# Attention by hash buckets with adapters: the last two pairs of heads interleaved by thirds of the queries, and a first pair prepared in another order

## The chip, the cores and the metric

The kernel runs on one core of a Trainium2 chip. The metric is the device time of one execution in microseconds (us). Eight runs of the kernel before are shown, and their median counts.

## What is computed

The first half is attention in which a query sees only the keys of its own hash bucket; the second half sends each row through two of eight small adapters and adds the result.

```python
q_bits = (np.einsum('bhsd,dk->bhsk', q, proj) > 0)       # 6 bits; the same for k
mask = q_bucket[:, :, :, None] == k_bucket[:, :, None, :]
scores = np.where(mask, scale * (q @ k.T), -1e9)
attn = softmax(scores); x = attn @ v                     # (4, 8, 768, 64) -> (3072, 512)
logits = x @ w_gate                                      # 8 experts, the best two, softmax over them
out = x + sum over the two experts e of w[e] * (x @ A[e]) @ B[e]     # rank 16
```

There are 4 batches of 8 heads, 768 positions and 64 features per head.

## The kernel before, in words

**Pairs and slots.** Two heads of a batch make a pair; there are 16 pairs (0 to 15), four to a batch. For each pair the scores are computed with the keys on the partitions, so that the exp of a score tile P is at once the stationary operand of the product with v. 2 heads x 6 key tiles x 768 queries are 9216 columns, cut into nine slots of 1024. `score` (L316) does one slot: three or four matmuls into a tile of the pool `ps_s` (two buffers of two PSUM banks), and one exp on ScalarE into `P_[p]`.

**The mask without a mask.** `aug` (L89, one of two buffers, alternating by pair) has 71 rows: 64 features, six signs of plus or minus one half, and one constant. Planes j = 0 to 3 are queries of head 0, keys of head 0, queries of head 1, keys of head 1. The score matmul over 71 rows falls far below zero wherever a bit differs; a small uniform term stands for rows that find no key (`uniform`, L354, with VectorE's add in `norm`, or for the last four pairs a matmul with the constant tile `eps`, L340).

**Preparing a pair.** `load_qk` and `load_v` queue loads on SyncE (SP). `trans` (L228) turns four blocks of 128x128 on TensorE into a PSUM bank and VectorE (or ScalarE) evicts them to `qkT`. `hash` (L252) makes the hash of all four planes in four column groups, VectorE takes the signs, and `sign_dma` (L163) moves them to rows 64 to 69 of `aug` by a transfer from SP's queue, one for each plane. `cast` (L272) fills rows 0 to 63 on GpSimd.

**Products.** `pvmm` (L334) multiplies P by v, six matmuls for each of six query tiles of a head, into a bank of `ps_v` (two banks); `norm` divides by the row sums and writes `x`, and GpSimd casts it to `xb`. `xturn` turns `xb` by a transfer, `xtrans` (L449) on TensorE with a copy on VectorE or ScalarE.

**Adapters.** `lgz` gives logits and the eight projections, `route_a` the maximum and the difference, `route_e` the exp of the router on ScalarE, `route_b` the weights and their product with the projections, `zmtrans` a transpose, `delta` the product with B, the sum with x and the store. `delta` ends either on VectorE or, with `by_pool`, on ScalarE (`tmp`) and GpSimd. A batch's six row tiles are done while the pairs of the next batch run; `moe_group` (L559) says which in which pair, `moe_slot` in which slot. For batch 2 they are (0, 1, 2) in pair 13 and (3, 4, 5) in pair 14.

**Order.** The whole order is written out by hand: the tile framework adds the waits between engines, but every engine runs its instructions as they are listed. `prologue` (L67) does head 0 and head 1 of pair 0, `first_pair` (L601) what lies beside its nine slots, `pair` (L630) what lies beside the slots of pairs 1 to 14, `last_pair` (L672) pair 15 and the tail. In pair 0, head 0's signs are written straight into `aug` by VectorE (`signs0`, L134), head 1's by `hash0` and two transfers. Pair 15's score columns are ordered so that two query tiles of both heads (a third of its queries) are complete after three slots; `third` (L389) does their product. The last third is done in two sixths after the last exp.

**Pools of one bank.** `ps_t` and `ps_m` have one bank each: an instruction that writes a new tile there waits until the last reader of the tile before is done.

Of the kernel before, what the change touches and what calls it, by code (L numbers as in the profile page):

```python
# [19 lines left out]
class Emitter:  # L20
# [46 lines left out]
    def prologue(self):  # L67
# [25 lines left out]
        self.qkT[0] = self.qktp.tile([P, 2 * S], F32, tag="qkT", name="qkT0")  # L93
        self.warm(19)
        self.turn0(0, self.ps_s, "s")
        self.half0(0, 0, nc.scalar.copy)
        self.half0(0, 1, nc.scalar.copy)
        self.signs0()
        self.turn0(1, self.ps_v, "v")
# [3 lines left out]
        self.half0(1, 0, nc.gpsimd.tensor_copy)  # L103
        self.half0(1, 1, nc.gpsimd.tensor_copy)
# [15 lines left out]
    def turn0(self, h, pool, tag):  # L120
        nc, P = self.nc, self.P
        for i in range(2):
            ps = pool.tile([P, 384], F32, tag=tag, name=f"trf{h}_{i}")
            for u in range(3):
                nc.tensor.transpose(out=ps[:, u * P:(u + 1) * P],  # L125
                                    in_=self.nat[0][:, i, h, u * P:(u + 1) * P], identity=self.ident)
            out = self.qkT[0][:, (2 * h + i) * 384:(2 * h + i + 1) * 384]
            if i:
# [5 lines left out]
    def signs0(self):  # L134
        nc, P = self.nc, self.P
        for i in range(2):
            hs = self.ps_s.tile([P, 2, 512], F32, tag="s", name=f"hsd{i}")
            for e in range(2):
                nc.tensor.matmul(out=hs[64:70, e, 0:384], lhsT=self.pst[64 * e:64 * e + 64, :],  # L139
                                 rhs=self.qkT[0][64 * e:64 * e + 64, i * 384:(i + 1) * 384],  # L140
                                 start=True, stop=True)
            nc.vector.tensor_scalar(out=self.aug[0][64:70, i, :].rearrange("p (e c) -> p e c", e=2),
                                    in0=hs[64:70, :, 0:384], scalar1=0.0, scalar2=0.5,
                                    op0=ALU.is_gt, op1=ALU.subtract)

    def hash0(self, h, engs):
        nc = self.nc
        hs = self.ps_t.tile([self.P, 384], F32, tag="t", name=f"hsf{h}")
        rows = slice(64 * h, 64 * h + 64)
        for i in (2 * h, 2 * h + 1):  # L150
            nc.tensor.matmul(out=hs[32 * i:32 * i + 32, :], lhsT=self.proj2,
                             rhs=self.qkT[0][:, i * 384:(i + 1) * 384], start=True, stop=True)
# [622 lines left out]
```

## Time and profile before

| | |
|---|---|
| median of 8 runs | 176.48 us (175.41 to 178.53) |
| profiled execution | 176.11 us, its span 174.3 us |
| granted TensorE clock | 0.988 |
| busy, TensorE and ScalarE | 161.9 and 150.8 us |
| busy, VectorE and GpSimd | 116.1 and 115.6 us |
| DMA | 28.51 MB, 164 GB/s on the mean |

A line of the page's groups has the source line, the engine, the operation, output and input with their shapes and the count, then the busy time, the mean of one in ns, and the idle time just before it with what ended it. A line of the timeline has start and duration in us, and merges equal instructions (x3) that follow each other; the idle time before the first stands in brackets. The span of 174.3 us ends with the landing of the last store.

### The profile page before, as it was taken

To read this page: it belongs to the slowest core of one execution; us is meant where nothing else is said; L and a number is where in the kernel's file an instruction comes from. 1 tells how busy PE (TensorE), PEld (TensorE's weight loads), DVE (VectorE), ACT (ScalarE), POOL (GpSimd) and SP (SyncE) were. 2 spreads that over 40 slices of the span, in tenths; PEclk is the share of its full clock that TensorE was granted. 3 is DMA by queue.
4 is the path that set the end of the run, shared out by engine and by line. 5 is a ranking of instruction groups with operands and counts; after the bars stand their busy time and mean duration, and the time that the engine had idled before them with its cause. 6 is when DMAs were issued, how large, how long until landed. Compare 5 with 4: busy or idle time off the path is not lost.

```text
span 174.3 us, 5249 instructions
## 1 busy us (share of the span) xinstructions
PE 161.9 (93%) x2100; PEld 112.1 (64%) x2105; DVE 116.1 (67%) x312; ACT 150.8 (87%) x176; POOL 115.6 (66%) x140
## 2 busy tenths in 40 slices
PE   7987999999999999999999999999999999998840
PEld 6454767675757676767667686767677676687610
DVE  3661747474746787878687786878785676647870
ACT  3666999999998899999997999999997988997760
POOL 8289969797897657575756677576766476630180
PEclk9999999999999999999999999999999999999995
DMA  5945499989897249687867268697964024250036
GB/s 145 338 151 188 123 259 147 188 153 184 145 210 222 73 114 224 212 168 262 134 221 211 88 144 295 134 197 235 160 219 150 4 53 182 41 198 4 2 125 236
DMA packets 30438, 28.51 MB, mean 164 GB/s; under 512 B 15078, under 2 KB 28494, under 8 KB 30414
## 3 DMA queue, kind: packets, MB, share of 16 engines
q1 hardware_dynamic: 25020, 27.38, 57.6%
q0 software_dynamic: 4832, 0.27, 4.7%
q10 hardware_dynamic: 562, 0.53, 0.9%
q8 instruction: 16, 0.26, 0.7%
q14 instruction: 8, 0.07, 0.1%
HBM read 19.42 MB, written 6.29 MB: 147 GB/s over the span
## 4 chain that ended last, share of the span: by engine, by line
PE 81%; DVE 6%; POOL 3%; issue 3%; ACT 2%; DMA 1%; POOLq 1%; ACTq 0%; DVEq 0%
PE s L323 33%; PE pv L330 18%; PE tr L238 13%; PE hs L258 7%; PE lz L475 4%; PE dl L543 1%; DMA nat<-in_q_dram 1%; PE xtp L458 1%; DVE xT L460 1%; ACT P L325 1%; POOL xb L385 1%; PE trf L125 1%; PE hsd L139 1%; PE ztp L529 1%; POOL acc L549 1%
## 5 line engine op out<-in xcount | busy, mean ns | idle before, releaser
L325 ACT ACTIVATE P<-s 128x1024 bf16<-128x1024 f32 x144 | 139.7, 1029 | 11.2 <-PE s L323 9.7
L323 PE MATMUL s<-aug 71*128 71x256 bf16 (+2 forms) x408 | 86.2, 316 | 1.2 <-ACT P L325 0.6
L276 POOL CAST aug<-qkT 64x1536 bf16<-64x1536 f32 x30 | 43.9, 1464 | 12.8 <-DVE qkT L245 10.1
L330 PEld LDWEIGHTS <-P 128*128 128x128 bf16 x1080 | 44.9, 98 | 11.3
L330 PE MATMUL pv<-vb,P 128*128 128x65 bf16 x1080 | 47.5, 193 | 0.2
L323 PEld LDWEIGHTS <-aug 71*128 71x128 bf16 x408 | 32.8, 97 | 19.2 <-issue 9.9
L245 DVE TENSOR_SCALAR qkT<-tr 128x512 f32<-128x512 f32 x40 | 27.4, 686 | 8.8 <-PE tr L238 8.3
L385 POOL CAST xb<-x 128x768 bf16<-128x768 f32 x15 | 12.4, 824 | 26.3 <-DVE x L379 23.9
L238 PE MATMUL tr<-ident,nat 128*128 128x128 f32 x180 | 28.3, 279 | 0.6 <-DVE xT L460 0.6
L238 PEld LDWEIGHTS tr<-ident,nat 128*128 128x128 f32 x180 | 20.1, 140 | 10.0 <-DVE qkT L245 3.1
L261 DVE TENSOR_SCALAR sgn<-hs 128x384 bf16<-128x384 f32 x15 | 8.4, 558 | 14.4 <-PE hs L258 12.9
L379 DVE TENSOR_TENSOR x<-pv,ri 128x384 f32<-128x384 f32 x30 | 16.7, 557 | 1.0
L551 DVE SCALAR_TENSOR_TENSOR acc<-dl,rt,x 128x512 f32<-128x512 f32 (+1 forms) x21 | 14.9, 719 | 3.1 <-PE dl L543 3.1
L221 POOL TENSOR_TENSOR vs<-vn 128x384 f32<-128x384 f32 x16 | 15.9, 995 | 0.0
L374 DVE TENSOR_TENSOR pv<-pv,uni 128x390 f32<-128x390 f32 x24 | 13.6, 566 | 2.5 <-PE pv L330 2.4
L219 POOL CAST vb<-vn 128x768 bf16<-128x768 f32 x16 | 13.2, 827 | 0.1
L258 PE MATMUL hs<-qkT,proj 128*32 128x384 f32 x120 | 12.8, 498 | 0.0
L549 POOL TENSOR_TENSOR acc<-tmp,x 128x512 f32<-128x512 f32 x4 | 5.0, 1264 | 8.8 <-ACT tmp L548 8.8
L475 PE MATMUL lz<-wa,xT 128*128 128x136 bf16 x96 | 9.3, 223 | 0.6 <-ACT xT L460 0.6
L543 PE MATMUL dl<-Bcat,zmT 128*128 128x512 bf16 x19 | 7.2, 381 | 1.1 <-ACT zmT L532 0.8
L361 DVE COPY uni<-un 128x130 f32<-128x130 f32 x12 | 3.5, 294 | 7.1 <-PE un L359 7.1
L224 POOL TENSOR_TENSOR vb<-vs,vs 128x128 bf16<-128x128 f32 x16 | 7.3, 458 | 1.3
(73 smaller groups left out, 122.4 us busy)
## 6 DMA issues: line engine op xcount, KB each, us to landing
vn<-in_v_dram SPq DMA_DIRECT2D x16, 384.0 KB
nat<-in_q_dram SPq DMA_DIRECT2D x15, 384.0 KB
nat<-in_k_dram SPq DMA_DIRECT2D x15, 384.0 KB
out_dram<-acc SPq DMA_DIRECT2D x4, 512.0 KB
out_dram<-acc SPq DMA_DIRECT2D x8, 256.0 KB
out_dram<-acc SPq DMA_DIRECT2D x2, 768.0 KB
aug<-sgn SPq DMA_DIRECT2D x60, 9.0 KB
nat<-in_q_dram SPq DMA_DIRECT2D x2, 192.0 KB
```

Of the source, the lines that this page charges most:

```text
L221: nc.gpsimd.tensor_add(out=s3, in0=vn[:, :, 0:3, :], in1=vn[:, :, 3:6, :])
L238: nc.tensor.transpose(out=ps[:, j * P:(j + 1) * P], in_=self.nat[p][:, idx % 2, idx // 2, u * P:(u + 1) * P], identity=self.ident)
L245: nc.vector.tensor_scalar(out=out, in0=ps, scalar1=2.0 ** -5, scalar2=None, op0=ALU.mult)
L258: nc.tensor.matmul(out=ps[32 * j:32 * j + 32, :], lhsT=self.proj2, rhs=self.qkT[p][:, j * 384:(j + 1) * 384], start=True, stop=True)
L276: self.nc.gpsimd.tensor_copy(out=self.aug[p % 2][0:64, :, e * n:(e + 1) * n], in_=self.qkT[p][64 * e:64 * e + 64, :].rearrange("p (j c) -> ...
L323: nc.tensor.matmul(out=ps[:, o:o + n], lhsT=aug[0:71, 2 * h + 1, kt * P:(kt + 1) * P], rhs=q, start=True, stop=True)
L325: nc.scalar.activation(out=self.P_[p][:, s * 1024:(s + 1) * 1024], in_=ps, func=ACT.Exp, scale=128.0)
L330: self.nc.tensor.matmul(out=pv, lhsT=self.p_at(p, h, kt, i), rhs=self.vb[p % 3][:, h, self.slot(kt), :], start=(start and kt == 0), stop=( ...
L379: nc.vector.tensor_tensor(out=self.x[b][:, :, c:c + D].rearrange("p (u e) d -> p e u d", e=2), in0=pv[:, 0:T, 0:D].rearrange("p (e u) d -> ...
L385: nc.gpsimd.tensor_copy(out=self.xb[b][:, hp], in_=self.x[b][:, :, hp * P:(hp + 1) * P])
L475: nc.tensor.matmul(out=lz[:, i, :], lhsT=self.xT[b][:, t, s * P:(s + 1) * P], rhs=self.wa[:, t, :], start=(t == 0), stop=(t == self.nD - 1))
L551: nc.vector.scalar_tensor_tensor(out=acc[:, i, c], in0=ps[:, c], scalar=self.rt[b, slots][:, i:i + 1], in1=self.x[b][:, slots[i], c], op0= ...
```

## The change

It has four parts.

1. *First pair.* `turn0`, `half0` and `hash0` become general. Head 1's signs of pair 0 go straight into `aug` too (`signs1` in slots 1 and 2, matmuls of 64x6 and VectorE), so that its two sign transfers and their hash fall away. The key signs of head 0 are taken in two instructions instead of one. The copies into `proj2` come ahead of the signs. Pair 1 is prepared head by head: `turn0` of head 0 in slot 3, its casts and `hash1` in slot 4, head 1 in slots 5 and 6, each hash with its two transfers.
2. *Pairs 1 to 13.* In pairs with two adapter tiles, one query tile of products moves from slot 1 to slot 5. `xtrans` of slot 8 uses `ps_m` instead of `ps_t`. Only pairs 14 and 15 take the uniform term from TensorE. Pair 13 has the adapter tiles (0, 1) of batch 2 only.
3. *Last two pairs.* Pairs 14 and 15 (p and q) run as 18 slots: p's first and second third, q's first and second, p's last, q's last. All of p and the first two thirds of q use `third`. Tiles (2, 3) of batch 2 stand in slots 0 to 7, tiles (4, 5) in slots 8 to 14, the last batch's tiles (0, 1) from slot 13, and the logits of its tiles (2, 3) in slot 16.
4. *Tail.* What slots 13 to 17 have done falls away there; the transposes of pair 14's last third are added.

The diff, cut to its core:

```diff
         self.warm(19)
-        self.turn0(0, self.ps_s, "s")
-        self.half0(0, 0, nc.scalar.copy)
-        self.half0(0, 1, nc.scalar.copy)
-        self.signs0()
-        self.turn0(1, self.ps_v, "v")
+        self.turn0(0, 0, [(self.ps_s, "s")] * 2)
+        self.half0(0, 0, 0, nc.scalar.copy)
+        self.half0(0, 0, 1, nc.scalar.copy)
         for e in range(2):
             nc.vector.tensor_copy(out=self.proj2[64 * e:64 * e + 64, e:12:2],
                                   in_=self.pst[64 * e:64 * e + 64, :])
-        self.half0(1, 0, nc.gpsimd.tensor_copy)
-        self.half0(1, 1, nc.gpsimd.tensor_copy)
+        self.signs0()
+        self.turn0(0, 1, [(self.ps_v, "v")] * 2)
+        self.half0(0, 1, 0, nc.gpsimd.tensor_copy)
+        self.half0(0, 1, 1, nc.gpsimd.tensor_copy)
...
     def signs0(self):
-        nc, P = self.nc, self.P
         for i in range(2):
-            hs = self.ps_s.tile([P, 2, 512], F32, tag="s", name=f"hsd{i}")
+            hs = self.ps_s.tile([self.P, 2, 512], F32, tag="s", name=f"hsd{i}")
             for e in range(2):
-                nc.tensor.matmul(out=hs[64:70, e, 0:384], lhsT=self.pst[64 * e:64 * e + 64, :],
-                                 rhs=self.qkT[0][64 * e:64 * e + 64, i * 384:(i + 1) * 384],
-                                 start=True, stop=True)
-            nc.vector.tensor_scalar(out=self.aug[0][64:70, i, :].rearrange("p (e c) -> p e c", e=2),
-                                    in0=hs[64:70, :, 0:384], scalar1=0.0, scalar2=0.5,
-                                    op0=ALU.is_gt, op1=ALU.subtract)
-    def hash0(self, h, engs):
+                self.hash0(i, e, hs[:, e, 0:384])
+            if i == 0:
+                self.sign0(i, hs[:, :, 0:384], 0, 2)
+            else:
+                for e in range(2):
+                    self.sign0(i, hs[:, e:e + 1, 0:384], e, e + 1)
+    def hash0(self, j, e, out):
+        self.nc.tensor.matmul(out=out[64:70], lhsT=self.pst[64 * e:64 * e + 64, :],
+                              rhs=self.qkT[0][64 * e:64 * e + 64, j * 384:(j + 1) * 384],
+                              start=True, stop=True)
+    def sign0(self, j, hs, e0, e1):
+        self.nc.vector.tensor_scalar(
+            out=self.aug[0][64:70, j, e0 * 384:e1 * 384].rearrange("p (e c) -> p e c", c=384),
+            in0=hs[64:70], scalar1=0.0, scalar2=0.5, op0=ALU.is_gt, op1=ALU.subtract)
+    def hash1(self, p, h):
         nc = self.nc
-        hs = self.ps_t.tile([self.P, 384], F32, tag="t", name=f"hsf{h}")
+        hs = self.ps_t.tile([self.P, 384], F32, tag="t", name=f"hsf{p}_{h}")
         rows = slice(64 * h, 64 * h + 64)
-        for i in (2 * h, 2 * h + 1):
-            nc.tensor.matmul(out=hs[32 * i:32 * i + 32, :], lhsT=self.proj2,
-                             rhs=self.qkT[0][:, i * 384:(i + 1) * 384], start=True, stop=True)
-        sgn = self.sgp.tile([self.P, 384], BF16, tag="sgn", name=f"sgnf{h}")
+        for j in (2 * h, 2 * h + 1):
+            nc.tensor.matmul(out=hs[32 * j:32 * j + 32, :], lhsT=self.proj2,
+                             rhs=self.qkT[p][:, j * 384:(j + 1) * 384], start=True, stop=True)
+        sgn = self.sgp.tile([self.P, 384], BF16, tag="sgn", name=f"sgnf{p}_{h}")
         nc.vector.tensor_scalar(out=sgn[rows], in0=hs[rows], scalar1=0.0, scalar2=0.5,
                                 op0=ALU.is_gt, op1=ALU.subtract)
-        for i in range(2):
-            self.sign_dma(engs[i], 0, 2 * h + i, sgn)
-    def half0(self, h, e, copy):
-        copy(out=self.aug[0][0:64, 2 * h:2 * h + 2, e * 384:(e + 1) * 384],
-             in_=self.qkT[0][64 * e:64 * e + 64, h * self.S:(h + 1) * self.S].rearrange("p (j c) -> p j c", j=2))
+        for j in (2 * h, 2 * h + 1):
+            self.sign_dma(nc.sync, p, j, sgn)
+    def signs1(self, j, banks):
+        hs = [pool.tile([self.P, 1, 384], F32, tag=tag, name=f"hsd{j}_{e}")
+              for e, (pool, tag) in enumerate(banks)]
+        for e in range(2):
+            self.hash0(j, e, hs[e][:, 0])
+        for e in range(2):
+            self.sign0(j, hs[e], e, e + 1)
+    def half0(self, p, h, e, copy):
+        copy(out=self.aug[p % 2][0:64, 2 * h:2 * h + 2, e * 384:(e + 1) * 384],
+             in_=self.qkT[p][64 * e:64 * e + 64, h * self.S:(h + 1) * self.S].rearrange("p (j c) -> p j c", j=2))
...
     def uni_pe(self, p):
-        return p >= self.n_pairs - self.PPB
+        return p >= self.n_pairs - 2
...
+    def third_out(self, p, u, fast=False):
+        b, hp, sl = self.B - 1, p % self.PPB, slice(2 * u, 2 * u + 2)
+        x, xb = self.x[b][:, :, hp * self.P:(hp + 1) * self.P], self.xb[b][:, hp]
+        if fast:
+            self.third_x(p, u, xb)
+        self.third_x(p, u, x)
+        if not fast:
+            self.nc.gpsimd.tensor_copy(out=xb[:, sl, :], in_=x[:, sl, :])
...
-        groups = ((0, 1), (2, 3), (4,), (5,)) if b < self.B - 2 else ((0, 1, 2), (3, 4, 5), (), ())
+        groups = ((0, 1), (2, 3), (4,), (5,)) if b < self.B - 2 else ((0, 1), (), (), ())
...
         if s == 0:
             self.load_qk(2)
-            self.hash0(1, (self.nc.sync, self.nc.sync))
             self.load_v(1)
             self.load_v(2)
-        if s < 3:
-            self.trans(1, s, bank=None if s == 1 else (self.ps_m, "m"))
+        if s == 1:
+            self.signs1(3, (T, M))
+        if s == 2:
+            self.signs1(2, (V, V))
         if s == 3:
-            self.cast(1, 0)
-            self.cast(1, 1)
+            self.turn0(1, 0, (T, M), on_act=False)
         if s == 4:
-            self.hash(1)
-            self.hash_b(1)
+            self.half0(1, 0, 0, self.nc.gpsimd.tensor_copy)
+            self.half0(1, 0, 1, self.nc.gpsimd.tensor_copy)
+            self.hash1(1, 0)
+        if s == 5:
+            self.turn0(1, 1, (M, V), on_act=False)
+            self.half0(1, 1, 0, self.nc.gpsimd.tensor_copy)
+            self.half0(1, 1, 1, self.nc.gpsimd.tensor_copy)
+        if s == 6:
+            self.hash1(1, 1)
+            self.load(3)
+            self.pvmm(0, 0, 0, 1)
+        if s == 7:
+            self.pvmm(0, 0, 1, 3)
+            self.trans(2, 0, bank=M)
             self.uniform(0)
-        if s == 5:
             self.vcast(1)
-            self.load(3)
-        if s == 6:
-            self.pvmm(0, 0, 0, 2)
-            self.trans(2, 0)
-        if s == 7:
-            self.pvmm(0, 0, 2, 4)
-            self.trans(2, 1, bank=(self.ps_m, "m"))
         if s == 8:
-            self.pvmm(0, 0, 4, 6)
+            self.pvmm(0, 0, 3, 6)
+            self.trans(2, 1)
             self.load_moe(0)
             self.load_moe(1)
     def pair(self, p, s):
+        n = len(self.moe_group(p)[1])
+        for at, i0, i1 in ((1, 0, 1), (3, 1, 3), (4, 3, 5), (5, 5, 6)) if n > 1 else ((1, 0, 2), (3, 2, 4), (4, 4, 6)):
+            if s == at:
+                self.pvmm(p - 1, 1, i0, i1)
...
             if p % self.PPB == 0:
-                self.xtrans(p - 1)
+                self.xtrans(p - 1, bank=(self.ps_m, "m"))
...
+    def last_two(self, p, q, b):
+        order = ((p, 0), (p, 1), (q, 0), (q, 1), (p, 2), (q, 2))
         t = [(0, 1), (2, 3), (4, 5)]
         x = self.x[b][:, :, (self.PPB - 1) * self.P:]
+        T2, c, far, one, free = 2 * self.T, b - 1, (self.ps_t, "t"), (self.ps_v, "v"), (self.ps_s, "s")
+        mid = (self.ps_m, "m")
+        for m in range(18):
+            j, u = order[m // 3]
+            self.score(j, 3 * u + m % 3)
+            if m == 0:
                 self.norm(p - 1, 0)
+                self.trans(q, 2)
+            for at, i0, i1 in ((1, 0, 1), (3, 1, 2), (4, 2, 4), (5, 4, 6)):
+                if m == at:
+                    self.pvmm(p - 1, 1, i0, i1)
+            if m == 1:
+                self.cast(q, 0)
+                self.cast(q, 1)
+            if m == 2:
+                self.hash(q)
+                self.hash_b(q)
+            if m == 6:
+                self.delta(c, t[1], 0)
                 self.norm(p - 1, 1)
+            if m == 7:
+                self.delta(c, t[1], 1)
+            if m == 9:
+                self.xturn(p - 1)
+            if m < 2:
+                self.lgz(c, t[1], (m,))
+            if m == 1:
+                self.route_a(c, t[1], now=False)
+            if m == 2:
+                self.route_e(c, t[1])
+            if m == 3:
+                self.route_b(c, t[1])
+            if m == 4:
+                self.zmtrans(c, t[1])
+            if m == 13:
                 self.lgz(b, t[0])
+                self.route_a(b, t[0], now=False)
+            for at, k in ((3, 0), (6, 1), (9, 2), (12, 3), (15, 4)):
+                if 0 <= m - at < 3:
+                    self.third(*order[k], m - at)
+                if m - at == 2 and k < 4:
+                    self.third_out(*order[k])
+            if m == 5:
+                self.vcast(q)
+            if m in (8, 9):
+                self.lgz(c, t[2], (m - 8,), bank=far)
+            if m == 9:
+                self.route_a(c, t[2], now=False)
+            if m == 10:
+                self.route_e(c, t[2])
+                self.route_b(c, t[2])
+            if m == 11:
+                self.zmtrans(c, t[2], bank=far)
+                self.xtrans(p, t[0], bank=mid)
+            if m == 12:
+                self.delta(c, t[2], 0, bank=far, by_pool=True)
+                self.xtrans(q, t[0], bank=mid)
+            if m == 14:
+                self.delta(c, t[2], 1, bank=far, by_pool=True)
+                self.route_e(b, t[0])
                 self.route_b(b, t[0])
+                self.xtrans(p, t[1], bank=far)
+            if m == 15:
+                self.xtrans(q, t[1], bank=far)
+            if m == 16:
+                self.lgz(b, t[1], bank=far)
+                self.route_a(b, t[1], now=False)
                 self.zmtrans(b, t[0])
+            if m == 17:
+                self.third_x(p, 2, self.xb[b][:, p % self.PPB])
+                self.third_x(p, 2, self.x[b][:, :, (p % self.PPB) * self.P:(p % self.PPB + 1) * self.P])
                 self.sixth(4, 0, 8)
+                self.delta(b, t[0], 0, bank=mid)
+        self.route_e(b, t[1])
         self.sixth(4, 8, T2)
         self.sixth_x(4, x)
+        self.xtrans(p, t[2], on_act=True, bank=free)
         self.sixth(5, 0, 4)
+        self.delta(b, t[0], 1, bank=mid, by_pool=True)
         self.sixth(5, 4, T2)
+        self.xtrans(q, (4,), on_act=True, bank=free)
         self.lgz(b, t[2], (0,), bank=one)
+        self.route_b(b, t[1], sums=False)
+        self.xtrans(q, (5,), on_act=True, bank=free)
         self.lgz(b, t[2], (1,))
+        self.zmtrans(b, t[1], on_act=True, bank=far)
         self.route_a(b, t[2])
         self.totals(b, t[1])
         self.delta(b, t[1], 0, by_pool=True)
```

Of `last_pair` the removed lines are left out above: it stood as in the kernel before, where it is printed in full.

## The prediction

> **What bounds the kernel now.** I read the page's busy shares first, then ScalarE's timeline alone, because one exp of 128x1024 per slot (nine slots a pair, 16 pairs) is the pulse of the kernel, then the waits, then the stretches around the three places that the diff touches.
>
> ```profile
> PE 161.9 (93%) x2100; PEld 112.1 (64%) x2105; DVE 116.1 (67%) x312; ACT 150.8 (87%) x176; POOL 115.6 (66%) x140
> ...
> L325 ACT ACTIVATE P<-s 128x1024 bf16<-128x1024 f32 x144 | 139.7, 1029 | 11.2 <-PE s L323 9.7
> ```
>
> Two engines are near full. An exp takes 1.03 us, but starts follow each other every 0.96 us (nine in 8.69 us below). So a gap in this train is lost time, and 9.7 of its 11.2 idle us are waits for the score matmuls.
>
> ```profile
> 8.99 1.02 ACT L325 ACTIVATE P<-s 128x1024 bf16<-128x1024 f32 x1 [0.59 <-PE s L323]
> 11.05 2.85 ACT L325 ACTIVATE P<-s 128x1024 bf16<-128x1024 f32 x3 [1.04 <-PE s L323]
> 14.18 1.02 ACT L325 ACTIVATE P<-s 128x1024 bf16<-128x1024 f32 x1 [0.28 <-PE s L323]
> 16.32 6.75 ACT L325 ACTIVATE P<-s 128x1024 bf16<-128x1024 f32 x7 [1.11 <-PE s L323]
> 23.23 8.69 ACT L325 ACTIVATE P<-s 128x1024 bf16<-128x1024 f32 x9 [0.17 <-PE s L323]
> ...
> 55.99 1.02 ACT L325 ACTIVATE P<-s 128x1024 bf16<-128x1024 f32 x1 [0.35 <-PE s L323]
> 57.47 2.07 ACT L325 ACTIVATE P<-s 128x1024 bf16<-128x1024 f32 x2 [0.46 <-PE s L323]
> ...
> 132.19 1.02 ACT L325 ACTIVATE P<-s 128x1024 bf16<-128x1024 f32 x1 [0.35 <-PE s L323]
> ...
> 143.23 1.02 ACT L325 ACTIVATE P<-s 128x1024 bf16<-128x1024 f32 x1 [0.53 <-PE s L323]
> ...
> 160.25 2.83 ACT L325 ACTIVATE P<-s 128x1024 bf16<-128x1024 f32 x3
> ```
>
> Read the starts. Pair 0 begins at 8.99 and pair 1 at 16.32 + 4 x 0.96 = 20.2, with 2.4 us of gaps. Pairs 1 to 4 take 8.86 us each. Pair 5 (as 9) has 0.81 us of gaps in its first two slots. Pair 13 takes 132.19 to 143.23, 11.04 us. Pairs 14 and 15 take from 143.23 to the end of the last exp at 163.08, 19.85 us. From there to the end of the span is a tail of 11.2 us.
>
> ```profile
> 147.25 3.15 SPq L164 DMA_DIRECT2D aug<-sgn  x4
> ```
>
> The sign rows of pair 15 leave SyncE's queue one by one, 0.78 us apart, the last issued at 149.6; pair 15 starts at 152.45, so nobody waits for them now.
>
> **What the Trainium skill says.** "Perfetto Trace Analysis", section Tensor Engine Instruction: the queues of ScalarE, VectorE and GpSimd are strict FIFO; "TensorE: Matmul & The Clock Gate", section Step-by-step, says matmuls keep program order. The trace agrees: at 56.11 a transpose waits for a copy, and the score behind it, whose inputs are ready, comes at 56.84. So every wait of TensorE is paid by the next score, which has only one spare buffer. "DMA: Bandwidth & Descriptors", section Anatomy of one DMA, gives a small transfer about 2 us of fixed cost. Here the second sign transfer of pair 0 is issued at 11.8 and the matmul that needs it runs at 13.74: 1.9 us, which I use. "TensorE: Matmul & The Clock Gate", Part 3, says that small matmuls in different row or column groups run concurrently: four hash matmuls take 0.78 us, and two take 0.77 us (9.15 to the transpose at 9.92), so it agrees.
>
> **The start.** It removes one transfer chain and adds TensorE work: head 1's signs by four matmuls of 64x6 (two pairs of 0.65 us if concurrent, as the second pair of L139 did from 6.17 to 6.82; 1.25 if in turn, as its first pair) for one hash of 0.77, and pair 1's hash as two of 0.70 for one of 0.78: +1.2 to +2.4 us. Placed in order: score 0 needs only the first half of the key signs, 7.87 instead of 8.26, so the first exp starts at 8.7. Scores 1 to 4 follow without large gaps, and the fifth exp starts at 12.6 (14.18 before). Then hash1 of head 0 waits for the two evictions of turn0, which VectorE reaches after the signs: 12.15 + 2 x 0.56 = 13.26. Hash 13.35 to 14.05, score to 14.5, sixth exp at 14.7: a gap of 1.1. At slot 6 hash1 of head 1 repeats it: evictions to 16.4, hash to 17.2, exp at 18.0, a gap of 1.3. Pair 0's products and the transposes of pair 2 (1.1 + 0.9 us of TensorE) now stand in its last three slots with no lead, and pair 1 starts at about 20.8. By its fourth slot it is 0.5 late. **+0.5**; from -0.3 (VectorE runs the signs ahead) to +1.3 (hashes in turn).
>
> **The middle.** xtrans at slot 8 of pairs 4, 8 and 12 moves from the bank that trans needs next to the one that lgz needs. Now trans waits until 56.11, though score 0 of pair 5 left TensorE at 55.73. Without that wait score 1 starts at 56.43 instead of 56.84, and its exp 0.40 earlier; the hash keeps it, since VectorE's eviction (57.27 to 57.95) lets it start at 58.02 instead of 58.41. 0.39 each. In pairs 6 and 10 six products (0.18 us) leave slot 1 for slot 5; the exp of slot 3 then follows the router's exp, 69.27 instead of 69.37: 0.1 each. Slot 5 has about 0.4 us of lead to hide them. Pair 13 has two adapter tiles instead of three, and 0.33 us of eps matmuls fewer; it becomes a pair like 9, which takes 104.2 - 94.11 = 10.06 before and 9.67 without its 0.39: -1.37, its bank included. VectorE's two uniform adds of 0.57 stand in its idle time, as in pair 9. Sum: 0.39 + 0.1 + 0.39 + 0.1 + 1.37 = **-2.35**; if pair 13 stays bound by TensorE, -1.6.
>
> **The last two pairs.** ScalarE's own work: 18 x 0.96 = 17.3, three router exps at 0.25 (a slot with one has 1.21), and, new here, two tmp activations of 0.69 that add 0.57 each: 19.2 us. TensorE has some 18.4 (scores 7.9, thirds 4.2, adapters 2.6, the rest 3.7), so it never leads by much. Time counted from pair 14's first exp:
> - Slots 1 to 5: 0.4 of gaps (hash, products and third together).
> - Slot 6 is pair 15's first, three slots earlier than before. Its signs end at 3.2; transfers are issued at 3.2, 4.0, 4.8, 5.6 and land at 5.1 to 7.5. Score 6 waits for the second, score 7 for the fourth: exps at 6.6 and 8.0, 0.75 lost. Behind the waiting scores stand delta and the third.
> - Slot 11: zmtrans comes one slot after its router exp. That exp runs at 11.8, its three VectorE operations end at 12.9; TensorE stands from 11.6, score 12 ends at 13.6, exp 12 starts at 13.8 instead of 13.1: 0.73. Slots 13 and 14 lose 0.2 to VectorE copies.
> - Slot 14: xtrans into the bank that tmp still has to read. tmp follows exp 14 and ends at 18.1; score 15 stands behind, exp 15 at 18.9 instead of 18.3: 0.6.
> - Slot 15: the next xtrans waits for a copy that VectorE does after the five router operations (19.3 to 19.6): 0.57. Slot 17: 0.3.
> Sum 19.2 + 3.55 = 22.7 against 19.85: **+2.85**; from 0 to +4. The thirds' bank costs nothing if the pool gives the one freed longest ago, as pair 6 shows (its products start at 72.10 while the other bank is divided until 72.40); otherwise 2.3 more at slot 6.
>
> **The tail.** One delta and the second group's logits are done earlier. But the chain after the last exp is what counts. VectorE arrives with two copies of the third (0.42 each) and one acc (0.74) in front of it, and sixth 5 waits for that acc through delta's bank: the last xb ends 2.2 us after the last exp (1.65 before), the last group's max starts at 3.26 (2.83 before). **+0.4**, from -0.8 (the removed work counts fully) to +1.
>
> **Sum**: +0.5 - 2.35 + 2.85 + 0.4 = +1.4. The profiled execution took 176.11 (span 174.3 and 1.8 around it), so 177.5; the median shown, 176.48, is 0.37 above that execution, so I give 177.9.
>
> **Rivals.** (a) It gets faster: the handovers in the last two pairs stay hidden because TensorE keeps its lead. For it: 18.4 us of TensorE against 19.2 of ScalarE, and pairs 6 and 7 hide similar handovers, two slots apart. Against: these are one slot apart, and the bank is shared. Hidden are then 0.75 + 0.73 + 0.6 + 0.57 + 0.3 = 2.95: 174.9. It decides when more than half of that is hidden; with start and tail at their better ends, 173.3. Chance 0.35. (b) Worse: hashes in turn (+0.8) and the sign transfers 1 us later, or the other bank: 179.7 to 180.4. Chance 0.2. (c) The interleaving holds but pair 13 gains little, 178.6; it counts with my forecast, 0.45 together.
>
> **Chances.** A measurement here can tell about 0.5% (0.9 us). Faster: (a) but its weakest part, and a little of mine, 0.37. Within: 0.16. Slower: 0.47. The range 173.4 to 180.4 spans (a) and (b); my case alone is 176.8 to 179.3.
>
> **What would show it.** Start: pair 1's first exp at 20.5 to 21, and gaps in front of the exps of slots 5 and 7. Middle: no transpose waiting for xT in pairs 5, 9, 13; pair 14 starting some 2 us earlier, near 141.4. Last pairs: ScalarE waiting for scores at slots 6, 7, 12, 15 and 16, and 22 to 23 us for both. If those gaps are missing and the two pairs take under 20.5 us, I am wrong and (a) is right.

## The result and the profile after

| | before | after |
|---|---|---|
| median | 176.56 us (32 runs) | 179.14 us (11 runs, 178.48 to 179.81) |
| ratio | | 1.015, interval 1.012 to 1.018 |
| profiled execution, its span | 176.11, 174.3 us | 179.28, 177.2 us |
| granted TensorE clock | 0.988 | 0.983 |

Some executions are granted a lower clock (in the kernel before 0.967 to 0.969, else 0.971 and more) and take 1% or more longer; the ratios leave them out (the medians don't), and of the profiled executions that are such (runs 1, 3 and 8 below) only stretches with a granted clock of 1.00 are read.

The change makes the kernel slower, by 2.9 us between the two profiled spans. The busy shares and the group of the exps, from the page of the kernel after:

```profile
PE 163.7 (92%) x2115; PEld 113.3 (64%) x2120; DVE 121.1 (68%) x330; ACT 152.3 (86%) x179; POOL 117.9 (67%) x146
...
L343 ACT ACTIVATE P<-s 128x1024 bf16<-128x1024 f32 x144 | 140.3, 1028 | 12.3 <-PE s L341 10.3
```

The exps have the same duration as before, and the idle time ahead of them grew only from 11.2 to 12.3 us. This sum hides the change: gaps went away in the middle and came up at both ends. ScalarE's timeline shows where:

```profile
9.08 5.12 ACT L343 ACTIVATE P<-s 128x1024 bf16<-128x1024 f32 x5 [0.28 <-PE s L341]
15.08 2.12 ACT L343 ACTIVATE P<-s 128x1024 bf16<-128x1024 f32 x2 [0.89 <-PE s L341]
18.08 1.02 ACT L343 ACTIVATE P<-s 128x1024 bf16<-128x1024 f32 x1 [0.89 <-PE s L341]
19.41 1.02 ACT L343 ACTIVATE P<-s 128x1024 bf16<-128x1024 f32 x1 [0.30 <-PE s L341]
21.16 1.02 ACT L343 ACTIVATE P<-s 128x1024 bf16<-128x1024 f32 x1 [0.73 <-PE s L341]
22.59 1.94 ACT L343 ACTIVATE P<-s 128x1024 bf16<-128x1024 f32 x2 [0.42 <-PE s L341]
24.92 8.69 ACT L343 ACTIVATE P<-s 128x1024 bf16<-128x1024 f32 x9 [0.39 <-PE s L341]
...
139.73 5.99 ACT L343 ACTIVATE P<-s 128x1024 bf16<-128x1024 f32 x6
...
149.56 1.03 ACT L343 ACTIVATE P<-s 128x1024 bf16<-128x1024 f32 x1 [0.43 <-PE s L341]
150.86 2.85 ACT L343 ACTIVATE P<-s 128x1024 bf16<-128x1024 f32 x3 [0.27 <-PE s L341]
153.97 1.02 ACT L343 ACTIVATE P<-s 128x1024 bf16<-128x1024 f32 x1 [0.26 <-PE s L341]
...
156.88 1.02 ACT L343 ACTIVATE P<-s 128x1024 bf16<-128x1024 f32 x1 [0.86 <-PE s L341]
...
161.72 1.02 ACT L343 ACTIVATE P<-s 128x1024 bf16<-128x1024 f32 x1 [0.70 <-PE s L341]
163.14 1.02 ACT L343 ACTIVATE P<-s 128x1024 bf16<-128x1024 f32 x1 [0.39 <-PE s L341]
164.42 1.02 ACT L343 ACTIVATE P<-s 128x1024 bf16<-128x1024 f32 x1 [0.26 <-PE s L341]
```

Four differences can be read from the starts. Pair 1's fourth exp comes at 24.92, before at 23.23: +1.69. Pair 14's first exp comes three steps of 1.0 after 139.73, at 142.72, before at 143.23: -0.5 in all, so the middle has won 2.2. The last two pairs end at 165.44, 22.72 us later; before they took 19.85: +2.87. The tail is 11.7 us, before 11.2: +0.5. The sum is +1.69 - 2.2 + 2.87 + 0.5 = +2.9. The first exp itself starts anywhere from 8.1 to 9.3 us in the profiled executions of this study, in unchanged prologues too (8.99 before, 9.34 in run 2), so the start is better counted from it: then it costs 1.60, not 1.69.

What TensorE waits for in the last two pairs is in the timeline of all engines there (the bracket is its idle time and the instruction that ended it):

```profile
146.04 3.15 SPq L182 DMA_DIRECT2D aug<-sgn  x4
...
148.84 0.34 PEld L341 LDWEIGHTS <-aug 71*128 71x128 bf16 x4 [0.28 <-issue]
...
150.43 0.11 PEld L341 LDWEIGHTS <-aug 71*128 71x128 bf16 x2 [0.45 <-DMA aug<-sgn]
...
156.01 0.28 PE L555 MATMUL ztp<-ident_bf,zm 128*128 128x128 bf16 x2 [1.14 <-DVE zm L534]
```

```profile
160.97 0.27 PE L484 MATMUL xtp<-ident_bf,xb 128*128 128x128 bf16 x2 [1.23 <-ACT tmp L574]
...
162.38 0.27 PE L484 MATMUL xtp<-ident_bf,xb 128*128 128x128 bf16 x2 [0.34 <-DVE xT L486]
```

Each of the three transposes waits for a result or for its bank, and the score behind it, which is ready, waits too: exps 12, 15 and 16 start 0.86, 0.70 and 0.39 late (slots are counted from pair 14's first).

The sign transfers hold TensorE twice. The second of the four is issued at 146.87 and the fourth at 148.47; the weights of score 6 load at 148.84 and those of the second half of score 7 at 150.43 (PEld), both 1.96 to 1.97 us after the issue. The first of these waits is labelled "issue", but the semaphores that the load waits for, until 148.81, are those of the first two transfers. TensorE's matmuls, which start 0.03 us apart in the third ahead of score 6 and 0.11 within score 7, pause for 0.38 and 0.44 us there. So the scores of slots 6 and 7 come 0.35 and 0.33 us late, which is nearly the whole of the gaps of 0.43 and 0.27 in front of their exps.

### The profile page after: what moved, and what is told of

It is laid out like the page before. It is cut to its first block, busy times and chain, and to the rows that moved or that the text cites. A ratio compares the mean times of both kernels' runs of the same rounds, so it can differ in the third digit from the quotient of the medians.

```text
span 177.2 us, 5312 instructions
## 1 busy us (share of the span) xinstructions
PE 163.7 (92%) x2115; PEld 113.3 (64%) x2120; DVE 121.1 (68%) x330; ACT 152.3 (86%) x179; POOL 117.9 (67%) x146
## 4 chain that ended last, share of the span: by engine, by line
PE 79%; DVE 10%; ACT 4%; POOL 2%; issue 2%; DVEq 0%; ACTq 0%; POOLq 0%
PE s L341 31%; PE pv L348 17%; PE tr L256 11%; PE hs L276 6%; PE hsd L147 2%; DVE qkT L263 2%; PE lz L501 2%; PE trf L126 2%; ACT P L343 2%; ACT tmp L574 1%; PE dl L569 1%; PE warm L202 1%; PE hsf L161 1%; PE ztp L555 1%; DVE pv L392 1%
## 5 line engine op out<-in xcount | busy, mean ns | idle before, releaser
L343 ACT ACTIVATE P<-s 128x1024 bf16<-128x1024 f32 x144 | 140.3, 1028 | 12.3 <-PE s L341 10.3
L348 PEld LDWEIGHTS <-P 128*128 128x128 bf16 x1008 | 42.8, 98 | 11.4 <-issue 0.6
L294 POOL CAST aug<-qkT 64x1536 bf16<-64x1536 f32 x28 | 41.0, 1464 | 11.5 <-DVE qkT L263 9.2
L348 PE MATMUL pv<-vb,P 128*128 128x65 bf16 x1008 | 45.5, 193 | 0.2
L263 DVE TENSOR_SCALAR qkT<-tr 128x512 f32<-128x512 f32 x37 | 25.3, 685 | 7.2 <-PE tr L256 3.7
L256 PE MATMUL tr<-ident,nat 128*128 128x128 f32 x168 | 26.4, 279 | 0.5 <-DVE qkT L263 0.3
L256 PEld LDWEIGHTS tr<-ident,nat 128*128 128x128 f32 x168 | 18.6, 140 | 7.9 <-DVE qkT L263 4.2
L392 DVE TENSOR_TENSOR pv<-pv,uni 128x390 f32<-128x390 f32 x28 | 15.9, 568 | 3.6 <-PE pv L348 3.6
L397 DVE TENSOR_TENSOR x<-pv,ri 128x384 f32<-128x384 f32 x28 | 15.6, 557 | 1.0
L575 POOL TENSOR_TENSOR acc<-tmp,x 128x512 f32<-128x512 f32 x5 | 6.3, 1266 | 8.6 <-ACT tmp L574 8.6
L241 POOL TENSOR_TENSOR vs<-vs 128x128 f32<-128x128 f32 x16 | 7.3, 457 | 1.3
```

The source lines that it names most:

```text
L256: nc.tensor.transpose(out=ps[:, j * P:(j + 1) * P], in_=self.nat[p][:, idx % 2, idx // 2, u * P:(u + 1) * P], identity=self.ident)
L263: nc.vector.tensor_scalar(out=out, in0=ps, scalar1=2.0 ** -5, scalar2=None, op0=ALU.mult)
L294: self.nc.gpsimd.tensor_copy(out=self.aug[p % 2][0:64, :, e * n:(e + 1) * n], in_=self.qkT[p][64 * e:64 * e + 64, :].rearrange("p (j c) -> ...
L343: nc.scalar.activation(out=self.P_[p][:, s * 1024:(s + 1) * 1024], in_=ps, func=ACT.Exp, scale=128.0)
L348: self.nc.tensor.matmul(out=pv, lhsT=self.p_at(p, h, kt, i), rhs=self.vb[p % 3][:, h, self.slot(kt), :], start=(start and kt == 0), stop=( ...
L392: nc.vector.tensor_tensor(out=pv[:, 0:T, :], in0=pv[:, 0:T, :], in1=self.uni[p][:, h:h + 1, :].to_broadcast([P, T, D + 1]), op=ALU.add)
```

## The experiments

Each ratio is to the kernel before, timed beside it. "Start" below is the time from the first exp of pair 0 to the fourth exp of pair 1: 14.24 before, 15.84 after.

**1. The changed kernel with the old first pair.**

```diff
-        self.turn0(0, 0, [(self.ps_s, "s")] * 2)
+        self.turn0(0, self.ps_s, "s")
...
+            self.trans(1, s, bank=None if s == 1 else (self.ps_m, "m"))
...
-            self.turn0(1, 0, (T, M), on_act=False)
```

> The changed kernel with the prologue and the first pair of the kernel before; the rest of the change stays. The changed kernel reaches pair 1's fourth exp at 24.92 us, the kernel before at 23.23. If the first pair's new order is a plain loss that nothing gives back, this one has the fourth exp of pair 1 at 23.2, pair 14's first at 141.0 and takes 1.7 us less than the changed kernel: 177.4, a ratio to before of 1.005. Rival: the late start is made good in the pairs bound by TensorE (5 to 13), which then have less to wait for; then pair 14 begins at 142.2 or later and the time is above 178.6.

Ratio 1.0061 (1.0026 to 1.0096). Against 1.015 the new first pair costs 0.9%, 1.6 us, as the starts say (15.84 - 14.24). The other parts together cost 0.6%. The rival is refuted: from pair 1's fourth exp to pair 14's first it is 117.79 us here and 117.80 in the changed kernel, so pairs 1 to 13 give nothing of a late start back.

**2. The middle alone, in the kernel before.**

```diff
+        for at, i0, i1 in ((1, 0, 1), (3, 1, 3), (4, 3, 5), (5, 5, 6)) if n > 1 else ((1, 0, 2), (3, 2, 4), (4, 4, 6)):
...
-            self.pvmm(p - 1, 1, 0, 2)
...
             if p % self.PPB == 0:
-                self.xtrans(p - 1)
+                self.xtrans(p - 1, bank=(self.ps_m, "m"))
```

> The kernel before with two edits of the change only: xtrans of slot 8 in the other bank, and one query tile of products moved from slot 1 to slot 5 in pairs with two or more adapter tiles. If the waits in pairs 5, 9 and 13 are what the trace says, the exps gain 0.39 us in each of pairs 5, 9 and 13 and 0.1 in pairs 6 and 10, and pair 14 begins 1.4 us earlier, near 141.9; nothing takes it back, and the time is 175.2, a ratio of 0.992. Rival: pairs 13 and 14 with three adapter tiles are bound by TensorE itself and swallow it; then pair 14 begins at 142.9 or later and the ratio is 0.997 or more.

174.92 us, ratio 0.9911 (0.9879 to 0.9943): **faster than both kernels.** Its ScalarE timeline in pairs 5, 13 and 14:

```profile
56.34 2.99 ACT L325 ACTIVATE P<-s 128x1024 bf16<-128x1024 f32 x3 [0.35 <-PE s L323]
59.79 2.86 ACT L325 ACTIVATE P<-s 128x1024 bf16<-128x1024 f32 x3 [0.22 <-PE s L323]
...
131.67 2.07 ACT L325 ACTIVATE P<-s 128x1024 bf16<-128x1024 f32 x2 [0.36 <-PE s L323]
...
142.40 2.12 ACT L325 ACTIVATE P<-s 128x1024 bf16<-128x1024 f32 x2 [0.61 <-PE s L323]
```

Pair 5's first and fourth exp before, for comparison, started at 55.99 (shown above) and at:

```profile
59.84 2.85 ACT L325 ACTIVATE P<-s 128x1024 bf16<-128x1024 f32 x3
```

Between the starts at 56.34 and 59.79 there are 3.45 us, before 3.85. What is gone is the gap of 0.46 ahead of the second exp, whose score stands behind the transposes that waited for their bank (0.21 us of TensorE at 56.11 before; here they don't wait). Only the bank edit reaches that place, since the moved products stand behind that score; for the rest of the pair no run separates the two edits. Of the 0.40, the whole of pair 5 keeps 0.32. Pair 13 keeps its three tiles and still takes 10.73 instead of 11.04. Counted from the first exp, pair 14 begins 1.2 us earlier than before, not 1.4 as expected; another 0.3 comes in pair 14 itself (9.60, before 9.91).

**3. The changed kernel with one transpose of pair 2 in the other bank.** In the changed kernel three tiles follow each other in `ps_t` (un, and two of `trans`), each waiting for VectorE.

```diff
-            self.trans(2, 1)
+            self.trans(2, 1, bank=M)
```

> The changed kernel, the second transpose group of pair 2 in slot 8 of pair 0 put into the free bank instead of the one that the uniform term has just used. One theory: three tiles in a row in that bank are what costs the last 1.2 us between pair 1's first and fourth exp; then the gaps of 0.73 and 0.42 before its first two exps fall to about 0.45 and 0, and its fourth exp comes at 24.1 or earlier, the time 178.3. The other: TensorE has no lead left and VectorE's norm holds the eviction that the hash waits for; then the first exps come earlier but the fourth only by 0.25, at 24.7, and the time is 178.9.

Ratio 1.0149 (1.0084 to 1.0213), no change that can be told, as the second theory had it. The trace shows what happens. ScalarE and TensorE at pair 1's first slots, one block for each view:

```profile
20.51 2.86 ACT L343 ACTIVATE P<-s 128x1024 bf16<-128x1024 f32 x3 [0.53 <-PE s L341]
24.27 8.69 ACT L343 ACTIVATE P<-s 128x1024 bf16<-128x1024 f32 x9 [0.91 <-PE s L341]
```

```profile
21.64 0.56 DVE L397 TENSOR_TENSOR x<-pv,ri 128x384 f32<-128x384 f32 x1
...
22.11 0.68 DVE L263 TENSOR_SCALAR qkT<-tr 128x512 f32<-128x512 f32 x1
22.84 0.85 PE L276 MATMUL hs<-qkT,proj 128*32 128x384 f32 x8 [0.66 <-DVE qkT L263]
```

The gap ahead of pair 1's second exp is gone and that ahead of the first has shrunk from 0.73 to 0.53, but the one at the fourth has grown from 0.39 to 0.91: start 15.63, only 0.21 less. The hash waits for an eviction that VectorE reaches after the three operations of `norm(0, 0)`. That VectorE's order is the wait behind the bank is only read from the trace here; the next run tries it.

**4. The same, with VectorE's order turned round in pair 1.**

```diff
         if s == 0:
-            self.norm(p - 1, 0)
+            if p > 1:
+                self.norm(p - 1, 0)
             self.trans(p + 1, 2)
+            if p == 1:
+                self.norm(p - 1, 0)
```

> The bank edit in slot 8 of pair 0 again, and in pair 1 alone the last transpose group of pair 2 ahead of the norm of pair 0's first head. With the bank alone the fourth exp of pair 1 came only 0.2 us earlier (seen against the first exp of the run), and the hash waited for VectorE's eviction, which stood behind the norm. If that order is the second half of the loss, the hash now follows its score at once and the fourth exp comes another 0.7 us earlier, 14.9 us behind the first exp of the kernel instead of 15.8: 178.2 us. Rival: TensorE, which has lost its lead over ScalarE in pair 0's last slots, sets the pace; then it comes less than 0.3 earlier and the time stays at 178.9.

178.06 us, ratio 1.0093 (1.0063 to 1.0123). Its ScalarE timeline:

```profile
8.08 5.11 ACT L343 ACTIVATE P<-s 128x1024 bf16<-128x1024 f32 x5 [0.28 <-PE s L341]
...
19.96 2.85 ACT L343 ACTIVATE P<-s 128x1024 bf16<-128x1024 f32 x3 [0.53 <-PE s L341]
22.99 8.69 ACT L343 ACTIVATE P<-s 128x1024 bf16<-128x1024 f32 x9 [0.17 <-PE s L341]
```

The start is 14.91, and the gap of 0.91 is 0.17 as in the kernel before. So VectorE's order accounts for 0.72 us, and bank and order together for 0.93 of the 1.60. The other 0.67 is there at pair 1's first exp: it starts 1.56 us after pair 0's last one, before 0.92, while up to pair 0's last exp the kernels are level (10.32 and 10.30 us after the first). TensorE's timeline between these two scores, here and before:

```profile
17.77 0.60 PE L341 MATMUL s<-aug 71*128 71x256 bf16 x3
18.21 0.71 PE L348 MATMUL pv<-vb,P 128*128 128x65 bf16 x18
18.83 0.66 PE L256 MATMUL tr<-ident,nat 128*128 128x128 f32 x4
19.32 0.60 PE L341 MATMUL s<-aug 71*128 71x512 bf16 x3
```

```profile
18.66 0.60 PE L323 MATMUL s<-aug 71*128 71x256 bf16 x3
19.09 0.53 PE L330 MATMUL pv<-vb,P 128*128 128x65 bf16 x12
19.46 0.60 PE L323 MATMUL s<-aug 71*128 71x512 bf16 x3
```

It works without a break: 18 products and a transpose group, 1.55 us from score to score, where before stood 12 products, 0.80. These are the products pushed to the end of pair 0. No run moves them back alone, so this share is read from the trace.

**5. Signs in place alone, in the kernel before.**

```diff
-            self.hash0(1, (self.nc.sync, self.nc.sync))
+            self.signs1(3, (self.ps_v, "v"))
...
+        if s == 1:
+            self.signs1(2, (self.ps_v, "v"))
```

> The kernel before with one half of the first part alone: head 1's signs of pair 0 go in place by four 64x6 matmuls in slots 0 and 1 (banks of the products' pool), its hash and two transfers fall away; pair 1 is prepared whole, as before. First theory (the start loses by pair 1's preparation head by head, its two short hashes behind evictions, and the products pushed to the end): this half costs nothing, pair 1's fourth exp starts 13.9 to 14.4 us after the first exp (before 14.24), ratio 0.998 to 1.001. Rival (the eight more TensorE and VectorE instructions of the signs are what pair 1 pays for): 0.6 us or more later, 14.9 or later, ratio 1.004.

Ratio 1.0013 (0.999 to 1.0035). Start 23.41 - 8.90 = 14.51, a little past the first theory's 14.4 and far from the rival's 14.9. In this kernel the signs in place cost 0.27 us, and all of it is there at pair 0's last exp (10.57 us after the first, before 10.30). In the changed kernel that exp comes at 10.33, so its 1.60 us are lost behind it, with pair 1 prepared head by head; the 0.27 can't simply be taken off them. The rival is refuted.

**6. Both transposes of the second thirds one slot later, so that `tmp` has left the bank.**

```diff
+            if m == 15:
                 self.xtrans(p, t[1], bank=far)
-            if m == 15:
+            if m == 16:
                 self.xtrans(q, t[1], bank=far)
-            if m == 16:
+                self.zmtrans(b, t[0])
+            if m == 17:
                 self.lgz(b, t[1], bank=far)
```

The logits of this group move from slot 16 to 17.

> The changed kernel, in the last two pairs: the transposes of the second thirds one slot later each (slots 15 and 16 instead of 14 and 15) and the logits of tiles 2 and 3 in slot 17 instead of 16, so that no score stands behind a transpose that waits for tmp to leave the bank or for VectorE's copy. If these handovers are what ScalarE waits for, the gaps of 0.70, 0.39 and 0.26 before exps 15 to 17 all but vanish and the last exp ends 1.2 us earlier, at 164.2; the tail grows by 0.3, since the logits come later: 178.2 us. Rival: the gaps only move, because TensorE is as full as ScalarE here; then the last exp ends at 165.2 and the time is 179 or more.

178.26 us, ratio 1.0098 (1.006 to 1.0137). The last exps:

```profile
161.06 1.94 ACT L343 ACTIVATE P<-s 128x1024 bf16<-128x1024 f32 x2
163.40 1.02 ACT L343 ACTIVATE P<-s 128x1024 bf16<-128x1024 f32 x1 [0.41 <-PE s L341]
```

The gaps at exps 15 and 16 (0.70 and 0.39) are gone, exp 17 has 0.41 where it had 0.26. The last two pairs take 21.54 us (142.88 to 164.42), 1.2 less, and the tail takes 12.2, 0.5 more. That the later logits are the cause was expected and is not shown.

**7. The second adapter group one slot earlier.**

```diff
-            if m in (8, 9):
-                self.lgz(c, t[2], (m - 8,), bank=far)
-            if m == 9:
+            if m in (7, 8):
+                self.lgz(c, t[2], (m - 7,), bank=far)
+            if m == 8:
                 self.route_a(c, t[2], now=False)
-            if m == 10:
+            if m == 9:
```

The router's exp then comes two slots ahead of the transpose of its result, not one.

> The changed kernel with the second adapter group (tiles 4 and 5 of batch 2) one slot earlier up to its weights: logits in slots 7 and 8, the router's exp and weights in slot 9; zmtrans stays in slot 11, now two slots behind the router's exp as everywhere else. If zmtrans standing one slot behind the router is what costs the 0.86 us in front of exp 12, that gap falls to 0.1 or less and the last exp ends 0.8 us earlier than in the changed kernel: 178.3 us. Rival: TensorE is full in slots 7 and 8 (products, third and delta) and the logits moved there delay scores 8 and 9 by as much; then gaps of 0.2 to 0.3 each appear before exps 8 and 9 and the time is 178.9 or more.

178.02 us, ratio 1.0102 (1.0062 to 1.0143). The exps 7 to 14:

```profile
150.43 3.08 ACT L343 ACTIVATE P<-s 128x1024 bf16<-128x1024 f32 x3 [0.27 <-PE s L341]
153.52 2.91 ACT L343 ACTIVATE P<-s 128x1024 bf16<-128x1024 f32 x3
156.89 1.96 ACT L343 ACTIVATE P<-s 128x1024 bf16<-128x1024 f32 x2
```

The gaps of 0.26 and 0.86 at exps 10 and 12 are gone. A part of the rival is there: exp 8 starts 1.14 us after exp 7, in the changed kernel 0.92, since the logits moved to slots 7 and 8; but exp 10 is already level again. The last two pairs take 21.67 us, 1.05 less.

**8. Old first pair with 6 and 7: all mends together.** Its diff is theirs.

> The changed kernel with all three repairs that touch whole parts: the first pair of the kernel before, the transposes of the second thirds one slot later, the second adapter group's router one slot earlier. If the effects add (1.6 + 0.9 + 0.8), it takes 175.8 us, a ratio to before of 0.996, and is still 0.9 us slower than the kernel before with the two middle edits alone, so that the interleaving itself has no gain left even when its waits are mended. Rival: with the waits gone the last two pairs run at ScalarE's pace and the interleaving pays; then it takes 174.9 or less.

Ratio 0.9971 (0.9937 to 1.0004). The three effects add, and this is still 0.6% behind the middle alone (run 2), with intervals that touch. Its ScalarE timeline around the last two pairs:

```profile
140.76 5.99 ACT L325 ACTIVATE P<-s 128x1024 bf16<-128x1024 f32 x6
...
163.22 1.02 ACT L325 ACTIVATE P<-s 128x1024 bf16<-128x1024 f32 x1 [0.41 <-PE s L323]
```

The two pairs take from 143.76 to 164.24, 20.48 us, what runs 6 and 7 together give (22.72 - 1.18 - 1.05). Pair 13, which has one adapter tile fewer, takes 9.65 us, so pairs 13 to 15 take 30.13; in run 2 they take 10.73 + 9.60 + 9.93 = 30.26. The tail, the same as in run 6, takes 12.1 us here and took 12.2 there, in run 2 11.2. So with its waits mended the interleaving is level with run 2 up to the last exp and loses 0.8 to 1.0 us behind it. No run mends the tail.

**9. Run 2's edits with batch 2's tiles spread over three pairs, without interleaving.** If the tiles taken out of pair 13 were the point, two of them each in pairs 13, 14 and 15 should be the cheap way to have it.

```diff
-        groups = ((0, 1), (2, 3), (4,), (5,)) if b < self.B - 2 else ((0, 1, 2), (3, 4, 5), (), ())
+        groups = ((0, 1), (2, 3), (4,), (5,)) if b < self.B - 2 else ((0, 1), (2, 3), (4, 5), ())
...
+            if s < 6:
+                self.moe_slot(p, s)
+            if s in (6, 7):
+                self.delta(b - 1, t[2], s - 6, bank=(self.ps_t, "t"))
```

The added lines stand in `last_pair`.

> The kernel before with the two middle edits (174.9 us alone) and batch 2's six adapter tiles spread as two each over pairs 13, 14 and 15 instead of three each over 13 and 14; pairs 14 and 15 stay one after the other. If the third tile is what made pairs 13 and 14 long, pair 13 falls from 10.7 to 9.7 and pair 14 from 9.6 to 9.1, pair 15 grows by at most 0.6 (it had 1.0 us of gaps), and the time is 173.9, a ratio to before of 0.985. Rival: pair 15 is the place where TensorE's and VectorE's short steps follow each other closely, and the tiles cost there what they save before; then pair 15 takes 11.4 us instead of 9.9 and the time is 174.9 or more.

176.71 us, ratio 0.9996 (0.9966 to 1.0026): the expectation was wrong and the rival holds. Pair 15 in the timelines of ScalarE and TensorE:

```profile
156.39 1.02 ACT L325 ACTIVATE P<-s 128x1024 bf16<-128x1024 f32 x1 [0.64 <-PE s L323]
...
161.03 1.02 ACT L325 ACTIVATE P<-s 128x1024 bf16<-128x1024 f32 x1 [0.88 <-PE s L323]
```

```profile
155.63 0.28 PE L529 MATMUL ztp<-ident_bf,zm 128*128 128x128 bf16 x2 [0.70 <-DVE zm L508]
...
160.17 0.38 PE L543 MATMUL dl<-Bcat,zmT 128*128 128x512 bf16 x1 [0.98 <-DVE acc L551]
```

Pair 13 takes 9.70 us and pair 14 takes 9.18, which saves 1.45 against run 2, and pair 15 takes 11.94 instead of 9.93, which loses 2.0; the tail loses 0.4. TensorE isn't full in pair 15: it stands 0.70 us before a transpose whose input VectorE still has to make, and 0.98 us before a delta whose bank VectorE still reads, and the exps behind come 0.64 and 0.88 late. These waits are of the kind that runs 6 and 7 took away; no run tried that here.

**10. The middle with the uniform term from TensorE in pairs 14 and 15 only.**

```diff
-        return p >= self.n_pairs - self.PPB
+        return p >= self.n_pairs - 2
```

> The middle part alone and, with it, the uniform term from TensorE in the last two pairs only. Theory: pair 13 with three adapter tiles is bound by TensorE, so the eps matmuls taken from it (0.33 us) come off the time: its exps take 10.4 us instead of 10.73, ratio 0.989. Rival (VectorE's uniform adds, 0.57 us each, come in front of evictions that TensorE waits for): 10.7 or longer, ratio 0.991 to 0.993.

174.70 us, ratio 0.9914 (0.989 to 0.9939). Pair 13 takes 10.31 us (131.35 to 141.66) and has its 0.4; pair 14 takes 9.97 instead of 9.60 and gives it back. The timeline of pair 14 says how:

```profile
147.40 0.57 DVE L374 TENSOR_TENSOR pv<-pv,uni 128x390 f32<-128x390 f32 x1 [0.26 <-PE pv L330]
...
148.71 0.74 DVE L551 SCALAR_TENSOR_TENSOR acc<-dl,rt,x 128x512 f32<-128x512 f32 x1
149.50 0.38 PE L543 MATMUL dl<-Bcat,zmT 128*128 128x512 bf16 x1 [0.25 <-DVE acc L551]
```

VectorE's uniform add for pair 13 stands in front of the first acc, and the second delta waits for this acc to leave its bank: the two deltas start 1.78 us apart, in run 2 1.37. From the first exp of pair 0 to the end of the last exp it is 152.6 us with and without the edit. Both theories were right, each for one pair.

**11. Run 10 with the signs in place.**

```diff
-        return p >= self.n_pairs - self.PPB
+        return p >= self.n_pairs - 2
...
-            self.hash0(1, (self.nc.sync, self.nc.sync))
+            self.signs1(3, (self.ps_v, "v"))
```

> The middle part with the uniform term from TensorE in the last two pairs only, and head 1's signs of pair 0 in place: the parts that should cost nothing or gain, without the interleaving and without pair 1 head by head. If the parts add: ratio 0.988 to 0.990. If the signs cost 0.6 us after all: 0.992 to 0.994.

174.72 us, ratio 0.9925 (0.9894 to 0.9956), between the two expectations and not to be told from run 10. Runs 2, 10 and 11 are the fastest kernels of the study and equal within their intervals. Run 2 is the one to keep, as the smallest edit.

## Why the prediction was right in sum, and where it was not

The forecast was 177.9, slower by 1.4; measured were 179.14 and +2.6 in the medians, inside the range. By its own steps:

**The start: the term that was mis-sized.** Forecast +0.5 (range -0.3 to +1.3), measured +1.69 (1.60 from the first exp), beyond the range, and nearly the whole of the error in the sum. The placement held up to pair 1's first exp. Counted from the first exp, forecast at 8.7 and measured at 9.08, the exps of slots 5 and 7 and pair 1's first were forecast 6.0, 9.3 and 12.1 us later and came 6.0, 9.0 and 12.1 later. At pair 1's first that is already 0.86 behind the kernel before, the products without a lead that the prediction named. It then says "By its fourth slot it is 0.5 late", as if the next slots made up time. They lose 0.74 more. Of the error of 1.2 us 0.4 is the start of the first exp, which differs as much between executions of one prologue, and 0.8 is in these three slots. Two things were not followed past that point: the pool `ps_t`, into which three tiles come in a row, and VectorE, to which pair 0's late products bring `norm` in front of the eviction that pair 1's hash needs. Runs 3 and 4 size them: 0.21 for the bank (already at pair 1's first exp), 0.72 for VectorE's order. The other 0.67 is the products and transposes in TensorE's way (run 4).

The hashes in turn, which rival (b) prices at +0.8, are not what happened, though the hash of two planes stands with 1.30 us, not 0.70:

```profile
13.20 1.30 PE L161 MATMUL hsf<-qkT,proj 128*32 128x384 f32 x4
13.66 0.14 PEld L161 LDWEIGHTS hsf<-qkT,proj 128*32 128x32 f32 x2 [0.33 <-DVE qkT L132]
```

The second plane's weights load at 13.66, when VectorE has evicted it, and its matmul ends 0.84 us later, at 14.50; the first plane's ran from 13.20 to 14.04. The Trainium skill ("TensorE: Matmul & The Clock Gate", Part 3), on which the 0.70 rested, says that matmuls placed in different tiles of the array run at once, and the trace agrees: the two overlap by 0.37 us, from when the second has its input. From the first exp the pair ends 5.42 us later, forecast 5.35. The price of 0.65 for two sign matmuls side by side was a misreading: the second pair of L139 shows 0.88 us before, and two of them show 0.81 after.

**The middle: right.** Forecast -2.35, measured -2.2. Pairs 5 and 9 gained 0.4 up to their fourth exp and kept 0.32 each (forecast 0.39), pairs 6 and 10 gained 0.11 each (0.1), pair 13 took 9.65 instead of 11.04, 1.39 less (1.37), and pair 12 lost 0.06. The 10.06 for pair 9 before should have been 9.97; the smaller gain of its bank made up for it.

**The last two pairs: right, as a sum and by place.** Forecast 22.7 us, measured 22.7. The gaps fell where they were placed: 0.43 + 0.27 at slots 6 and 7 (forecast 0.75), 0.86 at 12 (0.73), 0.70 at 15 (0.6), 0.39 at 16 (0.57), 0.26 at 17 (0.3). Run 7 took away the cause named for slot 12 and run 6 that for slots 15 and 16, and those gaps went, 1.05 and 1.18 us. At slots 6 and 7 score 6 did wait for the second sign transfer and score 7 for the fourth, 0.35 and 0.33 us by the trace; no run takes these waits away. Rival (a), that these handovers stay hidden, is refuted by the same gaps. (With start and tail at their better ends its own terms give 172.9, not 173.3; nothing hangs on it.)

**The tail: right.** Forecast +0.4, measured +0.5. The last xb ends 2.07 us after the last exp (forecast 2.2), the last group's max starts at 3.2 (forecast 3.26).

So the loss of 2.6 us has three shares: the first pair costs 0.9% (run 1 against the change), the interleaving with its tail, and with what leaves pairs 12 and 13 for it, costs 1.5% (run 1 against run 2), and the middle returns 0.9% (run 2). Of the interleaving's share the waits at slots 10 to 16 are shown by runs 6 and 7; what is left with both mended lies in the tail (run 8). Whether batch 2's tiles have room in pair 15 without interleaving stays open: run 9 lost there to two waits that it did not mend.

## What to carry to other kernels

When work is moved, follow each queue and each one-buffer pool until the old rhythm is back, not only until the moved work is done: here a place forecast to 0.1 us was followed by three slots that lost 0.74 more. In an engine that runs in order, a small step whose input is late also holds up the ready step behind it: the transpose of the second adapter group, one slot behind the exp of its router, put the next exp of the scores 0.86 us late, and with two slots between them that gap was gone. And try the parts of a change one by one: here two small edits of the middle alone were 0.9% faster than before, while the whole was 1.5% slower.

## What the runs showed that was not expected

- The 0.42 us that pair 13 gained when its uniform term went from TensorE to VectorE were lost in the pairs beside it (run 10): 152.6 us from first exp to last in both.
- Taking away the nearest wait moved most of the gap to the next one: 0.73 + 0.42 + 0.39 us of gaps in pair 1's first four exps became 0.53 + 0.91 (run 3).
- With its waits mended the interleaving takes as long as run 2 up to the last exp (pairs 13 to 15: 30.13 against 30.26 us), and what it still loses, 0.8 to 1.0 us, stands behind the last exp (run 8).
